# A second pair of token groups by block products one chunk earlier, and a last output tile in halves

## The chip, the cores and the metric

The kernel runs on one core of a Trainium2 chip. The metric is the device time of one launch in microseconds (us). Shorter is better. The engines are called PE (TensorE), DVE (VectorE), ACT (ScalarE), POOL (GpSimd) and SP (SyncE, which here only issues transfers).

## The reference

Attention under a block mask, then two feed-forward stages in float32. The change touches the last one alone:

```python
def _moe2_ref(x, g_ln, w_ch1, w_ch2):          # x: 4 x 576 x 512, w_ch1: 512 x 2048, w_ch2: 2048 x 512
    mu = np.mean(x, axis=-1, keepdims=True)
    var = np.mean((x - mu) ** 2, axis=-1, keepdims=True)
    xn = (x - mu) / np.sqrt(var + 1e-06) * g_ln
    ch = np.maximum(xn @ w_ch1, 0.0) @ w_ch2
    return (x + ch).astype(np.float32)
```

## The kernel before

A float32 matrix product is made as three passes over float32r operands: each operand is split into a high part and a low part (rounded value and remainder), and high x high, low x high and high x low are added up in PSUM.

**The last stage** has 2304 tokens in five groups: four of 512 tokens and one, Z, of 256. The hidden width of 2048 is cut into eight chunks `c` of 256 columns. For each chunk and group, `em_c1` makes the first product (weights `w_ch1`, 24 matmuls of the group's width), ACT takes the relu and DVE the remainder, and `em_c2` makes the second product, one output tile of 128 tokens at a time: six matmuls of 512 columns into a PSUM bank `po` (there are three), which DVE adds to the tile `acc` in SBUF (line 896). In the last chunk each `acc` tile is stored right behind that addition.

**Seven products.** Two groups of 512 tokens form a pair: P is groups 0 and 3, Q is groups 2 and 1. The first product of a pair and a chunk can be seen as a 2x2 block matrix times a 2x2 block matrix. `em_c1s` does it with seven block products of six matmuls (42) in place of eight (48), with sums of the inputs (`SF`, four tiles s0 to s3, each with high and low parts and two halves k) and sums of the weight blocks (`TF`, tiles ta and tb, high part 0 and low part 1). It goes through two plain products, s0 with weight sums, s3 with a plain weight block, s1 with weight sums, then the output tiles of the group before, s2 with weight sums, two output tiles, and a plain input block with weight sums. Its results are put together by three ACT copies and four DVE additions.

**The sums of the inputs** don't depend on the chunk. POOL makes them (`sum_forms`: f1, f2, f3, f4 for s0, s1, s2, s3; 5, 4, 5 and 4 operations for one half k). SBUF holds one pair's `SF` at a time; the other's are kept in DRAM (`s_scr`). Those of P are made in chunks 0 and 1. P goes by seven products from chunk 2 on, Q from chunk 5 on, and in chunks 2 to 4 Q goes plainly by `em_c1`. In these three chunks `sums_for` (line 1320) makes Q's sums a part at a time: when P's seven products are through, the buffer of `TF` is given to POOL as scratch, POOL writes its sums over a part of P's in `SF`, stores them to `s_scr`, loads P's part back, and only then the buffer can take the weight sums of the next chunk. From chunk 5 on `em_c1s` reloads the other pair's `SF` behind each product (`reload`, 1 MB each); chunk 6 has its own second buffer for the weight sums (`TF[6]`, tb).

**What sets the order.** The order is written out by hand; each engine takes its instructions as they stand. Loading and splitting a chunk's weights is cut into steps (`chunk_jobs`, a list of turns). `tick` takes one turn at fixed places among the matmuls. A chunk with one pair by seven products has 17 ticks, one with two has 16. In the list, `forms` makes the four weight sums, `t_high` (ACT) their high part and `t_low` (DVE) the low part; `high` and `low` are the same for a weight piece. Four empty turns stand ahead of the list where the chunk at hand is 2, 3 or 4.

Of the kernel before, what the change touches and what calls it, by code (L numbers as in the profile page):

```python
# [7 lines left out]
F32 = mybir.dt.float32  # L8
# [4 lines left out]
ALU = mybir.AluOpType  # L13
# [10 lines left out]
NC2 = DFF2 // CF  # L24
# [8 lines left out]
def attention_moe_kernel(ctx, tc, raw_d, dup_d, raw0_d, dup0_d, v_d, v0_d, msk_d, mz_d, vec_d, eye_d, wk_d, wv_d, wr_d, wc1_d, wc2_d, out_d):  # L33
    nc = tc.nc
# [327 lines left out]
    def mm(out, lhsT, rhs, start, stop=True, **kw):  # L362
        nc.tensor.matmul(out=out, lhsT=lhsT, rhs=rhs, start=start, stop=stop, **kw)  # L363
# [275 lines left out]
    W = [None, None]  # L639
    TF, XN, SF = {}, {}, []  # L640

    def chunk_jobs(c):
        L, kept = [], []
        for k in (0, 2):
            w = wc1_d[128 * k:128 * k + 256, CF * c:CF * c + CF].rearrange("(a p) n -> p a n", a=2)
            L.append(load_split(w, lambda i, k=k: W[c % 2][0][i][:, k:k + 2], kept))
        for k in range(2):
            r0 = CF * c + 128 * k
            L.append(piece(wc2_d[r0:r0 + 128], lambda i: W[c % 2][1][i], k))
        if c == 0:  # L650
            return L
        z = []

        def forms():
            (b11, b12), (b21, b22) = [[st["a2"].rearrange("p (a n) -> p a n", a=2)[:, :, o:o + 128] for o in (0, 128)] for st in kept]
            raw = stg2.tile([128, 4096], I8, name="raw8")
            z.append(raw.bitcast(F32).rearrange("p (i a n) -> p i a n", i=4, a=2))
            z1, z2, z3, z4 = [z[0][:, i] for i in range(4)]
            for out, in0, in1 in ((z1, b12, b11), (z3, b22, b12), (z2, b22, z1), (z4, b21, z2)):
                tt(out=out, in0=in0, in1=in1, op=ALU.subtract)  # L660

        load, above, below, expo, bits, high, low = [list(x) for x in zip(*[(l, a1, a2, x, b, h, w) for l, (a1, a2), (x, b), h, w in L])]
        low = [lambda f=f: f(nc.vector) for f in low]
        if c == 1:
            return [
                [load[0], load[1]],
                [above[0], below[0]],
                [expo[0], bits[0]],
                [high[0], above[1], below[1], load[2]],
                [expo[1], bits[1]],  # L670
                [high[1], above[2], below[2], low[0], load[3]],
                [expo[2], bits[2]],
                [low[1], high[2], above[3], below[3]],
                [expo[3], bits[3]],
                [low[2], high[3]],
                [low[3]],
            ]
        t_high, t_low = lambda: act(TF[c][0], z[0]), lambda: sub(nc.vector, TF[c][1], z[0], TF[c][0])
        return [
            [load[0], load[1]],  # L680
            [above[0], below[0]],
            [expo[0], bits[0]],
            [high[0], above[1], below[1], load[2]],
            [expo[1], bits[1]],
            [high[1], above[2], below[2], low[0], load[3]],
            [expo[2], bits[2]],
            [forms, above[3], below[3], high[2]],
            [expo[3], bits[3], t_high],
            [low[1], low[2]],
            [high[3], t_low],  # L690
            [low[3]],
        ]

    def chunk_tiles(p):
        return [p.tile([128, 4, CF], F32R, name=f"c1{i}") for i in range(2)], [p.tile([128, 2, DM], F32R, name=f"c2{i}") for i in range(2)]
# [112 lines left out]
    def dma_sums(pr, out, ii, k=slice(0, 2)):  # L808
        for i in ii:
            m, s = s_scr[PAIRS.index(pr), i][:, :, k], SF[i][:, :, k].bitcast(F32)  # L810
            nc.gpsimd.dma_start(out=m if out else s, in_=s if out else m)
# [69 lines left out]
        split(w, 0, b)  # L881
        em_c2(c, g0, (2, 3))

    def em_c2(c, G, ts):
        t0, n = groups[G]
        h1 = T["h1", c, G]
        w2 = W[c % 2][1]
        for t in ts:
            if t >= n // 128:
                continue  # L890
            i = t0 // 128 + t
            p = po.tile([128, 512], F32, name="po")
            for x, (hi_, wi) in enumerate(((0, 0), (0, 1), (1, 0))):
                for m in range(2):
                    mm(p, h1[hi_][:, m, 128 * t:128 * t + 128], w2[wi][:, m], m == 0 and x == 0, m == 1 and x == 2)
            tt(out=acc[i], in0=p, in1=acc[i], op=ALU.add)  # L896
            if c == NC2 - 1:
                nc.sync.dma_start(out=out_d[128 * i:128 * i + 128], in_=acc[i])

# [11 lines left out]
    with tc.manual_schedule():  # L913
# [376 lines left out]
        def open_sums(pr):  # L1290
            T["et"] = ExitStack()
            return sum_forms(pr, opened(T["et"], "tz", 4, side=R))
# [20 lines left out]
        def forms_for(*cc):  # L1313
            T["et"].close()
            T["ef"] = ExitStack() if len(cc) == 1 else es_f
            ta = tf_tiles(opened(T["ef"], "ft", side=R), "ta")
            for c in cc:
                TF[c] = ta

        def sums_for(c):  # L1320
            del TF[c]
            T["ef"].close()
            f1, f2, f3, f4, _ = open_sums(Q)
            if c == 2:
                for k in (0, 1):
                    f3(k)
            else:
                for f in (f1, f2, f4):
                    f(c - 3)
            ii, k = ((2,), slice(0, 2)) if c == 2 else ((0, 1, 3), c - 3)  # L1330
            for pr, out in ((Q, True), (P, False)):
                dma_sums(pr, out, ii, k)
            forms_for(*((c + 1,) if c < 4 else (5, 7)))

        def tick():
            if turns:
# [13 lines left out]

        for c in range(1, NC2):
            if c + 1 < NC2:
                more = chunk_jobs(c + 1)
                if c == 1:
                    turns[0:0] = turns1
                    turns += [[] for _ in range(15 - len(turns))]
                    for x, t in enumerate(more):
                        turns[3 + x] = turns[3 + x] + t
                else:
                    turns += [[] for _ in range(4 * (c < 5))] + more  # L1360
            if c == 1:
                for G in (P[1], P[0], Z, *Q):
                    todo = group(c, G, todo)
                continue
            one, two = (Q, P) if c == 6 else (P, Q)
            em_c1s(c, one, two if c > 4 else None, [lambda ts=ts, x=todo: em_c2(*x, ts) for ts in ((0, 1), (2, 3))], tick)
            if c < 5:
                sums_for(c)
            tick()
            todo = group(c, Z, (c, one[1]))  # L1370
            if c < 5:
                for G in Q:
                    todo = group(c, G, todo)
            else:
                em_c1s(c, two, None, [lambda: em_c2(c, Z, (0, 1))], tick)
                todo = c, two[1]
                tick()
            if c == 4:
                del XN[g3, 0], T["o1"]
                es_o.close()  # L1380
                TF[6] = tf_tiles(opened(es_f, "fb"), "tb")
        em_c2(*todo, range(4))


# [64 lines left out]
```

## Time and profile before

| | us |
|---|---|
| median of three runs | 830.64 (829.98 to 833.07) |
| the profiled execution, its own time | 830.76 |
| its span | 828.9 |
| PE busy in it | 799.6 |
| DVE, ACT, POOL busy | 560.7, 413.9, 333.5 |
| chunks 2 to 7 of the last stage | from about 532 to the end |

The share of busy time is an average over stages. In the last stage PE takes a matmul of 512 columns every 0.23 us almost without a gap, so this stage is read by where PE stands at a time and by what must have arrived by then.

### The profile page before, as it was taken

The page shows a single profiled execution, that of the slowest core. Times are in us where ns is not written, and L with a number is a line of the kernel's source. Part 1 is how long each engine was busy: PE and PEld are TensorE (multiplying, and loading weights), DVE is VectorE, ACT ScalarE, POOL GpSimd, SP SyncE. Part 2 cuts the span into 40 slices and gives each one's busy share as a digit, 9 for nine tenths or more (in the row PEclk, how much of TensorE's full clock was granted, in tenths as well). Part 3 has the DMA queues.
Part 4 walks back from the last instruction along what each step waited for, and adds up shares of the span by engine and source line. Part 5 has one row for each costly group of instructions (what it writes and reads, how often), then busy time and mean ns, then how long its engine had stood idle before and what let it go on. Part 6 is the DMA issues. An engine that isn't in the chain of part 4 may idle for free.

```text
span 828.9 us, 10597 instructions
## 1 busy us (share of the span) xinstructions
PE 799.6 (96%) x3774; PEld 662.9 (80%) x3774; DVE 560.7 (68%) x1014; ACT 413.9 (50%) x706; POOL 333.5 (40%) x294
## 2 busy tenths in 40 slices
PE   4999899899999999999999999999999999999998
PEld 3766766678898998998988887888888888878886
DVE  6898799886788324144386669768576667758545
ACT  6887688878786533535544423233241335243211
POOL 5796789857574011011021669442080730010100
PEclk9999999999999999999999999999999999999999
DMA  8998788721351110012434111604034166160433
GB/s 221 321 338 235 223 253 256 232 94 77 126 211 45 52 64 29 10 39 77 153 110 157 51 52 52 253 26 173 6 113 141 51 207 249 52 239 16 152 153 127
DMA packets 47636, 112.60 MB, mean 136 GB/s; under 512 B 5408, under 2 KB 19872, under 8 KB 45280
## 3 DMA queue, kind: packets, MB, share of 16 engines
q1 hardware_dynamic: 37792, 64.40, 24.2%
q0 software_dynamic: 9360, 45.17, 16.1%
q10 hardware_dynamic: 432, 2.36, 0.7%
q8 instruction: 30, 0.49, 0.2%
q14 instruction: 22, 0.18, 0.1%
HBM read 91.62 MB, written 20.30 MB: 135 GB/s over the span
## 4 chain that ended last, share of the span: by engine, by line
PE 79%; DVE 12%; ACT 5%; issue 2%; DMA 1%; POOL 0%; ACTq 0%; DVEq 0%
PE s L363 23%; PE ph L363 22%; PE po L363 21%; PE p L363 12%; DVE part L418 4%; ACT r L41 2%; ACT e L41 1%; DVE QK L451 1%; DVE a L135 1%; PE ph L714 1%; DMA V<-in_v_dram 1%; DVE acc L896 1%; DVE m L449 1%; DMA raw<-in_raw_dram 1%; ACT h L41 1%
## 5 line engine op out<-in xcount | busy, mean ns | idle before, releaser
L363 PE MATMUL po<-c,h 128*128 128x512 f32 x864 | 207.9, 393 | 1.4 <-DVE acc L896 0.8
L363 PEld LDWEIGHTS po<-c,h 128*128 128x128 f32 x864 | 161.0, 188 | 39.3 <-DVE acc L896 5.0
L363 PE MATMUL ph<-x,c 128*128 128x512 f32 (+1 forms) x552 | 116.6, 353 | 0.0
L896 DVE TENSOR_TENSOR acc<-po,acc 128x512 f32<-128x512 f32 x144 | 94.6, 684 | 23.3 <-PE po L363 22.5
L363 PEld LDWEIGHTS ph<-x,c 128*128 128x128 f32 x552 | 91.4, 188 | 15.3
L363 PE MATMUL p<-e,V 128*128 128x512 f32 (+1 forms) x310 | 91.1, 441 | 0.0
L363 PE MATMUL p<-wv,k 128*128 128x512 f32 x360 | 82.9, 390 | 0.0
L363 PEld LDWEIGHTS p<-e,V 128*128 128x128 f32 x310 | 55.3, 192 | 31.8 <-issue 26.9
L363 PEld LDWEIGHTS p<-wv,k 128*128 128x128 f32 x360 | 67.4, 188 | 13.8
L41 ACT ACTIVATE h<-ph 128x512 fp32r<-128x512 f32 (+1 forms) x53 | 28.3, 534 | 89.1 <-PE ph L363 89.1
L44 DVE TENSOR_TENSOR k<-a,k 128x768 fp32r<-128x768 f32 x24 | 23.0, 958 | 72.2 <-ACT a L41 72.2
L418 DVE TRANSPOSE_TENSOR_REDUCE part<-s 128x14 f32<-128x448 f32 (+4 forms) x160 | 65.1, 467 | 2.7 <-PE s L363 1.8
L41 ACT ACTIVATE a<-raw,ce 128x512 f32<-128x512 int8 (+1 forms) x76 | 54.7, 753 | 17.5 <-DVE a L135 10.9
L41 ACT ACTIVATE u<-ph 128x512 f32<-128x512 f32 x27 | 16.1, 598 | 87.5 <-PE ph L363 86.2
L41 ACT ACTIVATE e<-s 128x1536 f32<-128x1536 f32 (+1 forms) x34 | 48.4, 1424 | 15.3 <-PE s L363 10.1
L363 PE MATMUL s<-y,wk 128*128 128x384 f32 x288 | 51.4, 338 | 0.0
L363 PE MATMUL s<-x,wk 128*128 128x384 f32 x288 | 51.2, 338 | 0.0
L363 PEld LDWEIGHTS s<-y,wk 128*128 128x128 f32 x288 | 50.7, 188 | 0.5 <-DVE r L629 0.3
L363 PEld LDWEIGHTS s<-x,wk 128*128 128x128 f32 x288 | 50.8, 188 | 0.2
L814 POOL DMA_DIRECT2D s<-s_scr x12 | 6.4, 535 | 107.9 <-PE ph L363 107.9
L41 ACT ACTIVATE a<-s 128x768 f32<-128x768 f32 x24 | 19.5, 813 | 58.6 <-PE s L363 58.6
L44 POOL TENSOR_TENSOR kq<-raw,kq 64x512 fp32r<-64x512 f32 x31 | 40.1, 1293 | 21.3 <-DMA kq<-in_dup_dram 15.8
(177 smaller groups left out, 1388.9 us busy)
## 6 DMA issues: line engine op xcount, KB each, us to landing
kq<-in_dup_dram POOLq DMA_DIRECT2D x15, 1088.0 KB, 6.9
s<-s_scr POOLq DMA_DIRECT2D x13, 1024.0 KB, 7.4
raw<-in_raw_dram SPq DMA_DIRECT2D x32, 288.0 KB, 5.7
raw<-in_w_ch_dram SPq DMA_DIRECT2D x16, 511.6 KB, 3.6
raw<-in_w_ch_dram SPq DMA_DIRECT2D x32, 255.6 KB, 3.6
V<-in_v_dram SPq DMA_DIRECT2D x16, 320.0 KB, 5.6
s_scr<-s POOLq DMA_DIRECT2D x5, 1024.0 KB, 6.3
x_scr<-r SPq DMA_DIRECT2D x18, 256.0 KB, 2.0
```

The lines of the kernel that those rows point to most:

```text
L41: nc.scalar.activation(out=out, in_=in_, func=func, **kw)
L44: eng.tensor_tensor(out=out, in0=in0, in1=in1.bitcast(F32), op=ALU.subtract)
L135: stt(out=st["a2"].bitcast(I32), in0=w3, scalar=5, in1=st["a1"].bitcast(I32), op0=ALU.logical_shift_right, op1=ALU.bitwise_or)
L363: nc.tensor.matmul(out=out, lhsT=lhsT, rhs=rhs, start=start, stop=stop, **kw)
L418: red(out=pt[0:kp, b0:b0 + w // 32, j], in_=v3(s[0:kp, o:o + w]), axis=AX.X, op=ALU.max, apply_transpose=True)
L449: lambda: red(out=m, in_=r4[0:32, :, 0:ng], axis=AX.X, op=ALU.max),
L451: lambda x=x: tt(out=v3(dst)[:, x:x + 16], in0=m[:, x:x + 16].unsqueeze(2).to_broadcast([32, 16, 32]), in1=s[64:96, 512:544].unsqueeze(1). ...
L714: nc.tensor.transpose(out=pt[kk][:, 128 * x:128 * x + 128], in_=z[:, 128 * kk:128 * kk + 128], identity=eye)
L814: nc.gpsimd.dma_start(out=SF[i].bitcast(F32), in_=s_scr[PAIRS.index(pr), i])
L896: tt(out=acc[i], in0=p, in1=acc[i], op=ALU.add)
```

## The change

Chunk 4 does both pairs by seven products, as chunks 5 to 7 did before. So Q's sums have to be done in chunks 2 and 3: `sums_for` makes all four sums of one half k in each of them, in the order s0, s1, s3, s2, and stores each as it is done; P's part of each is loaded back one step later. The weight sums of chunks 3 and 4 (`late`) are split at the end of the list, in turns 12 and 13, since POOL holds their buffer longer. The second buffer tb now serves chunks 5 and 7, and the pair that comes first is Q in chunks 5 and 7. In the last chunk the last output tile is made, added and stored in two halves of 256 columns.

```diff
@@ chunk_jobs(c, late=False)
-            [expo[3], bits[3], t_high],
+            [expo[3], bits[3]] + [t_high] * (not late),
             [low[1], low[2]],
-            [high[3], t_low],
-            [low[3]],
-        ]
+            [high[3]] + [t_low] * (not late),
+            [low[3]] + [t_high] * late,
+        ] + [[t_low]] * late
@@ em_c2(c, G, ts, halves=())
+            cols = (slice(0, 256), slice(256, 512)) if t in halves else (slice(0, 512),)
+            for y in cols:
+                p = po.tile([128, 512], F32, name="po")[:, y]
...
+                tt(out=acc[i][:, y], in0=p, in1=acc[i][:, y], op=ALU.add)
+                if c == NC2 - 1:
+                    nc.sync.dma_start(out=out_d[128 * i:128 * i + 128, y], in_=acc[i][:, y])
@@ sums_for(c)
-            if c == 2:
-                for k in (0, 1):
-                    f3(k)
-            else:
-                for f in (f1, f2, f4):
-                    f(c - 3)
-            ii, k = ((2,), slice(0, 2)) if c == 2 else ((0, 1, 3), c - 3)
-            for pr, out in ((Q, True), (P, False)):
-                dma_sums(pr, out, ii, k)
-            forms_for(*((c + 1,) if c < 4 else (5, 7)))
+            for i, f, back in ((0, f1, ()), (1, f2, (0,)), (3, f4, (1,)), (2, f3, (3, 2))):
+                f(c - 2)
+                dma_sums(Q, True, (i,), c - 2)
+                dma_sums(P, False, back, c - 2)
+            forms_for(*((3,) if c == 2 else (4, 6)))
@@ the loop over chunks
-                more = chunk_jobs(c + 1)
+                more = chunk_jobs(c + 1, c in (2, 3))
...
-                    turns += [[] for _ in range(4 * (c < 5))] + more
+                    turns += [[] for _ in range(4 * (c < 4))] + more
...
-            one, two = (Q, P) if c == 6 else (P, Q)
-            em_c1s(c, one, two if c > 4 else None, ...
-            if c < 5:
+            one, two = (Q, P) if c in (5, 7) else (P, Q)
+            em_c1s(c, one, two if c > 3 else None, ...
+            if c < 4:
                 sums_for(c)
...
-            if c == 4:
+            if c == 3:
...
-                TF[6] = tf_tiles(opened(es_f, "fb"), "tb")
-        em_c2(*todo, range(4))
+                TF[5] = TF[7] = tf_tiles(opened(es_f, "fb"), "tb")
+        em_c2(*todo, range(4), (3,))
```

On PE, in chunk 4, where Q's first group begins (x_3733 and x_3734 are its high and low inputs, c_3726 and c_3727 the chunk's weights), before:

```order
L363 MATMUL ph<-x_3733,c_3726 128x512 x4
L363 MATMUL ph<-x_3733,c_3727 128x512 x4
L363 MATMUL ph<-x_3734,c_3726 128x512 x4
L363 MATMUL ph<-x_3733,c_3726 128x512 x4
L363 MATMUL ph<-x_3733,c_3727 128x512 x4
L363 MATMUL ph<-x_3734,c_3726 128x512 x4
```

and with the change (s_3908 is s0, s_3732 is s3, ta_5376 and ta_5377 the weight sums):

```order
L363 MATMUL ph<-x_3733,c_3726 128x512 x2
L363 MATMUL ph<-x_3733,c_3727 128x512 x2
L363 MATMUL ph<-x_3734,c_3726 128x512 x2
L363 MATMUL ph<-x_3733,c_3726 128x512 x2
L363 MATMUL ph<-x_3733,c_3727 128x512 x2
L363 MATMUL ph<-x_3734,c_3726 128x512 x2
L363 MATMUL ph<-s_3908,ta_5376 128x512 x2
L363 MATMUL ph<-s_3908,ta_5377 128x512 x2
L363 MATMUL ph<-s_3908,ta_5376 128x512 x2
L363 MATMUL ph<-s_3732,c_3726 128x512 x2
L363 MATMUL ph<-s_3732,c_3727 128x512 x2
L363 MATMUL ph<-s_3732,c_3726 128x512 x2
```

The plain products of whole groups have become block products, which read s0 and s3 of Q and the weight sums of chunk 4.

On POOL, at the end of its work in chunk 3 (t are scratch tiles; a row with s on the left of s_scr's arrow is a store, the other way round a load), before:

```order
L44 TENSOR_TENSOR s3_3732<-t_5336,s3_3732 128x512
L811 DMA s_scr_78<-s0_3908 256x1x512
L811 DMA s_scr_78<-s1_3909 256x1x512
L811 DMA s_scr_78<-s3_3732 256x1x512
L811 DMA s0_3908<-s_scr_78 128x2x512
L811 DMA s1_3909<-s_scr_78 128x2x512
L811 DMA s3_3732<-s_scr_78 128x2x512
```

and with the change:

```order
L44 TENSOR_TENSOR s3_3732<-t_5355,s3_3732 128x512
L811 DMA s_scr_78<-s3_3732 256x1x512
L811 DMA s1_3909<-s_scr_78 128x2x512
L765 TENSOR_TENSOR t_5363<-x201_3734,o1_3917 128x512
L765 TENSOR_TENSOR t_5362<-x200_3733,o1_3917 128x512
L765 TENSOR_TENSOR t_5362<-t_5362,t_5363 128x512
L777 TENSOR_SCALAR s2_3910<-t_5362 128x512
L44 TENSOR_TENSOR s2_3910<-t_5362,s2_3910 128x512
L811 DMA s_scr_78<-s2_3910 256x1x512
L811 DMA s3_3732<-s_scr_78 128x2x512
L811 DMA s2_3910<-s_scr_78 128x2x512
```

The sum s2 now stands between the store of s3 and the load that brings P's s3 back, and the three loads no longer stand together.

On ACT, at the end of chunk 3 (raw_5470 and raw_5495 hold the weight sums, c_3728 is a weight piece of chunk 4), before:

```order
L41 ACTIVATE c_3728<-a_5431 128x512
L41 ACTIVATE ta_5351<-raw_5470 128x1024
L41 ACTIVATE h_5499<-ph 128x512 x2
L41 ACTIVATE c_3728<-a_5477 128x512
L41 ACTIVATE u<-ph 128x512
```

and with the change:

```order
L41 ACTIVATE c_3728<-a_5456 128x512
L41 ACTIVATE h_5523<-ph 128x512 x2
L41 ACTIVATE c_3728<-a_5502 128x512
L41 ACTIVATE ta_5376<-raw_5495 128x1024
L41 ACTIVATE u<-ph 128x512
```

The high part of the weight sums has moved behind the last weight split, to the place in front of the next chunk's first copy `u`.

## Rows read from the trace of the kernel before

**Rows 1.** The page's head: span, and PE's busy time, share and instructions.

```profile
span 828.9 us, 10597 instructions
PE 799.6 (96%) x3774; PEld 662.9 (80%) x3774; DVE 560.7 (68%) x1014; ACT 413.9 (50%) x706; POOL 333.5 (40%) x294
```

**Rows 2.** Waits of PE's weight loads, 520 to 829 us: total, times, longest.

```profile
PEld po L363 <- DVE acc L896: 3.7, 8, 0.5
```

**Rows 3.** Timeline of PE, chunks 4 and 5: start, us, line, operation, out<-in, count.

```profile
629.00 2.92 PE L363 MATMUL ph<-x,c 128*128 128x512 f32 x12
631.76 1.54 PE L363 MATMUL ph<-s,ta 128*128 128x512 f32 x6
633.13 1.52 PE L363 MATMUL ph<-s,c 128*128 128x512 f32 x6
...
658.33 5.62 PE L363 MATMUL ph<-x,c 128*128 128x512 f32 x24
...
677.47 2.91 PE L363 MATMUL ph<-x,c 128*128 128x512 f32 x12
...
706.92 2.93 PE L363 MATMUL ph<-x,c 128*128 128x512 f32 x12
...
724.90 2.92 PE L363 MATMUL ph<-x,c 128*128 128x512 f32 x12
```

**Rows 4.** Instructions by form, 520 to 829 us: busy us, mean ns | idle before.

```profile
L363 PE MATMUL ph<-x,c 128*128 128x256 f32 x144 | 18.0, 281 | 0.0
...
L741 DVE SCALAR_TENSOR_TENSOR h<-ph,h 128x256 fp32r<-128x256 f32 x12 | 4.9, 418 | 2.3 <-ACT h L41 2.1
```

**Rows 5.** Timeline of POOL, chunk 2 (550) and chunk 3 (598 on).

```profile
550.48 2.58 POOL L765 TENSOR_TENSOR t<-x,o 128x512 f32<-128x512 f32 x2 [23.78 <-PE ph L363]
...
557.12 2.58 POOL L765 TENSOR_TENSOR t<-x,o 128x512 f32<-128x512 f32 x2
...
598.95 2.58 POOL L765 TENSOR_TENSOR t<-o,x 128x512 f32<-128x512 f32 x2 [29.13 <-PE ph L363]
...
605.60 2.67 POOL L765 TENSOR_TENSOR t<-t,x 128x512 f32<-128x512 f32 x2
...
610.95 1.84 POOL L765 TENSOR_TENSOR t<-x,t 128x512 f32<-128x512 f32 x1
...
616.87 2.14 POOL L811 DMA_DIRECT2D s_scr<-s  x3
```

**Rows 6.** The same view in chunk 1, P's second half of sums.

```profile
505.39 3.49 POOL L765 TENSOR_TENSOR t<-s,x 128x512 f32<-128x512 f32 x2
...
512.96 3.29 POOL L765 TENSOR_TENSOR t<-t,x 128x512 f32<-128x512 f32 x2
```

**Rows 7.** Transfers of the whole span: count, KB each, median us from issue to landing.

```profile
raw<-in_w_ch_dram SPq DMA_DIRECT2D x32, 255.6 KB, 3.6
...
s<-s_scr POOLq DMA_DIRECT2D x6, 512.0 KB, 7.9
...
n_scr<-RT SPq DMA_DIRECT2D x7, 16.0 KB, 1.7
```

**Rows 8.** The same view, 549 to 580 us alone.

```profile
s<-s_scr POOLq DMA_DIRECT2D x1, 1024.0 KB, 5.2
```

**Rows 9.** The transfers of `s_scr`, 598 to 632 us; the least is the first store's.

```profile
DMA to landing us min/median/max: 3.2/6.4/9.0
```

**Rows 10.** Timeline of ACT at the start of chunk 4; idle before it in brackets.

```profile
630.58 0.60 ACT L41 ACTIVATE u<-ph 128x512 f32<-128x512 f32 x1 [5.75 <-PE ph L363]
```

**Rows 11.** Timeline of DVE at the start of chunk 4.

```profile
629.20 0.69 DVE L896 TENSOR_TENSOR acc<-po,acc 128x512 f32<-128x512 f32 x1 [0.64 <-PE po L363]
632.03 0.69 DVE L852 TENSOR_TENSOR u<-ph,u 128x512 f32<-128x512 f32 x1 [2.14 <-PE ph L363]
```

**Rows 12.** Timeline of DVE at the end of the kernel.

```profile
825.08 0.69 DVE L896 TENSOR_TENSOR acc<-po,acc 128x512 f32<-128x512 f32 x1 [0.67 <-PE po L363]
```

**Rows 13.** Instructions on the tile `acc`, 800 to 829 us: its stores.

```profile
DMA to landing us min/median/max: 2.0/2.0/4.0
```

More of the change, by code (lines that the diff above doesn't have):

```diff
@@ L640, in attention_moe_kernel, with chunk_jobs @@
     TF, XN, SF = {}, {}, []
-    def chunk_jobs(c):
+    def chunk_jobs(c, late=False):
         L, kept = [], []
@@ L882, in em_c1s, with em_c2 @@
         em_c2(c, g0, (2, 3))
-    def em_c2(c, G, ts):
+    def em_c2(c, G, ts, halves=()):
         t0, n = groups[G]
@@ L891, in em_c2 @@
             i = t0 // 128 + t
[L892 to L898, printed above, removed]
+            cols = (slice(0, 256), slice(256, 512)) if t in halves else (slice(0, 512),)
+            for y in cols:
+                p = po.tile([128, 512], F32, name="po")[:, y]
+                for x, (hi_, wi) in enumerate(((0, 0), (0, 1), (1, 0))):
+                    for m in range(2):
+                        mm(p, h1[hi_][:, m, 128 * t:128 * t + 128], w2[wi][:, m, y], m == 0 and x == 0, m == 1 and x == 2)
+                tt(out=acc[i][:, y], in0=p, in1=acc[i][:, y], op=ALU.add)
+                if c == NC2 - 1:
+                    nc.sync.dma_start(out=out_d[128 * i:128 * i + 128, y], in_=acc[i][:, y])
     PIECES = [
@@ L1364, in attention_moe_kernel @@
                 continue
-            one, two = (Q, P) if c == 6 else (P, Q)
-            em_c1s(c, one, two if c > 4 else None, [lambda ts=ts, x=todo: em_c2(*x, ts) for ts in ((0, 1), (2, 3))], tick)
-            if c < 5:
+            one, two = (Q, P) if c in (5, 7) else (P, Q)
+            em_c1s(c, one, two if c > 3 else None, [lambda ts=ts, x=todo: em_c2(*x, ts) for ts in ((0, 1), (2, 3))], tick)
+            if c < 4:
                 sums_for(c)
@@ L1370, in attention_moe_kernel @@
             todo = group(c, Z, (c, one[1]))
-            if c < 5:
+            if c < 4:
                 for G in Q:
```

## The prediction

> **What bounds the kernel now.** The page comes first: TensorE (PE) is busy 799.6 of 828.9 us [rows 1]. The waits view of the last stage comes next, for the engine's weight loads, where its stalls show: 3.7 us in eight pieces, none over 0.5 us, all for VectorE freeing an output bank [rows 2]. So in this stage the time is the number of matmuls times their pace, and any other engine matters only where it makes PE wait. The PE timeline then gives the pace [rows 3]. Chunk 4 runs from 629.00 to 677.47, 48.47 us; chunk 5, which already does both pairs by seven products, from 677.47 to 724.90, 47.43 us. The reader should note in it where a chunk first reads a sum or a weight sum: 631.76 (first sums times weight sums) and 633.13 (fourth sums, called s3, times a plain weight block). These two times are the deadlines of everything that the change puts at the end of the chunk in front. Last I read the GpSimd (POOL) timeline of chunks 2 and 3 and the landing times of the transfers, since the change loads that engine and its queue.
>
> **Part 1: pair Q in chunk 4 by seven products.** The plain pair takes 48 matmuls, the seven products 42. Before, from 658.33 to 677.47 (the Q part of chunk 4) there are 84 matmuls with the output tiles between them, 19.14 us, 0.228 us each; the same part of chunk 5, from 706.92 to 724.90, has 78 in 17.98 us, 0.2305 each [rows 3]. That is 1.16 us less by this stretch and 1.04 us less by whole chunks, against 6 x 0.228 = 1.37 us if every matmul kept the plain pace; the rest goes to the slightly slower pace of the form. I take 1.04, since chunk 4 will be in the order that chunk 5 has now, with everything that the form adds: three ScalarE copies, four VectorE additions and four reloads of 1 MB on POOL's queue. All of that is thus paid for in the 47.43 us. Chunks 5 to 7 keep their counts; only which pair comes first is swapped, which I cost at nothing. The weight sums of chunks 5 and 7 now go to the second buffer, also nothing.
>
> **Part 2: sums by halves in chunks 2 and 3.** This is where it can be lost. Before, POOL makes 10 operations in chunk 2, 13 in chunk 3 and 13 in chunk 4; now 18 in chunk 2, 18 in chunk 3 and none in chunk 4. It can start only when PE has read the last weight sum, because the scratch tiles lie in that buffer: 598.95 in chunk 3. The four sums take, from the starts of neighbouring rows, 6.65 (605.60 less 598.95), 5.35, 5.92 and, for the one of chunk 2, 6.64 us [rows 5]: 24.6 us. In between stand five DMA issues of about 0.7 us (the three in a row at 616.87 take 2.14 [rows 5]), 3.6 us. So the last sum is done at 598.95 + 24.6 + 3.6 = 627.1, ten us later than the 616.87 of before. Then come the store of that sum (to 627.8), the reload of s3 (issued 627.8) and the reload of s2, which waits for the store in front of it.
>
> Who waits for that? First, the high half of the next weight sums on ScalarE needs the third operation of the last sum, about 624.4. The change puts it behind the last weight split, where ScalarE now idles 5.75 us before its next work at 630.58 [rows 10]. One operation of about 1 us fits there and nothing behind it is late. Second, the low half on VectorE now stands behind the last output addition, 629.20 + 0.69, and so ends about 631.1 (its 1.2 us estimated as twice a 128x512 operation). Behind it VectorE has nothing until 632.03 [rows 11]; PE wants it two matmuls after 631.76, at 632.2. Free, with 1.1 us to spare. Third, the staging buffer that the low half reads is freed some 5 us later, and the next load of weights on SP's queue with it: issued 631.1, median 3.6 us [rows 7], so there by 635. Chunk 4 reads it after 54 matmuls, 629.0 + 54 x 0.228 = 641.3. Free. Fourth, and closest, s3: its reload of 512 KB is issued at 627.8 and PE wants it at 633.13, so 5.3 us are left. No row shows such a load alone. The nearest rows are the 1 MB load with nothing beside it, 5.2 us [rows 8], which is the same kind at twice the size; below, the fastest 512 KB store, 3.2 us [rows 9]; above, the 512 KB loads as they are now, three in a batch with weights beside them, median 7.9 us [rows 7]. Now it has one store in front of it and, until the low half of the weight sums is done, no weights beside it. I take 4.2, between 3.2 and 5.2: there at 632.0, 1.1 us early. So 0 for each of the two boundaries (chunk 2 to 3 and 3 to 4), with 2.6 us each at 7.9. A gain is excluded, since PE has no wait there today. The reload of s2 is issued about 631, and its product stands behind 30 + 24 matmuls, 12 us into the chunk: at 7.9 us it is still in time.
>
> The DMA page of the Trainium skill ("DMA: Bandwidth & Descriptors", section "Anatomy of one DMA") gives about 2.0 us plus the bytes at 436 GB/s for a transfer that GpSimd issues: an estimate of 3.2 us here. The store's 3.2 us agrees with it, the loads' 7.9 us do not. By that rule s3 is there at 631.0 and the slow rival below would be gone; I keep the rival for the row's sake.
>
> **Part 3: the last output tile in halves.** It replaces 6 matmuls of 512 columns by 12 of 256. Those of 256 columns take 18.0 / 144 = 0.125 us each [rows 4], so 1.50 against 1.37 us; if they kept the plain pace, half of 0.228, nothing: I take +0.07. The last addition (825.08, 0.69 us [rows 12]) becomes one of 128x256, nearest row 0.418 [rows 4]: -0.27. The last store of 256 KB lands after 2.0 us [rows 13], one of 16 KB after 1.7 [rows 7]: 0 to -0.3 for 128 KB, I take -0.1. The first half's addition and store lie beside the second half's matmuls. Sum -0.30, from -0.57 to -0.14.
>
> **The sum.** -1.04 + 0 - 0.30 = -1.34 us. The profiled execution took 830.76 us (span 828.9 and 1.86 around it), so 829.42; the median of the runs shown is 830.64, 0.12 lower: 829.3 us.
>
> **Rivals.** (a) POOL's sums take longer because they now lie beside more VectorE work. For it: the same first sum took 7.57 us in the crowded stretch of chunk 1 (505.39 to 512.96 [rows 6]) against 6.65. Nearly 0.9 more for one sum, half of that for each of the others: some 2 us in all. Then s3 arrives at 634.0, PE waits 0.9 us at each boundary, +1.8: 831.1 us. Against it: by 617 most of a chunk's VectorE work is done. The page "SBUF — State Buffer" of the Trainium skill (section "SBUF: two separate sides") states that a VectorE operation with two SBUF inputs and a GpSimd operation that reads SBUF take the shared port pair by an exclusive lock, the other blocking for the whole instruction. The longer sum agrees with that; by the rule this rival is likelier the more VectorE work lies after 617. (b) The slow one: the reload of s3 takes what reloads take now, 7.9 us, so 635.7 and a wait of 2.6 us at two boundaries, +5.2, which eats the gain: 834.5 us; with (a) on top 4.6 each, 838.5. The place is the product of PE's 633.13 row, in chunk 4 and in chunk 3; it begins to cost from 5.3 us on and turns the change slower than before from 6.0. For it: the 7.9 row. Against it: the batch, which is now broken up. (c) The change doesn't do what it says: six matmuls go, but the second pair's chain of additions holds PE up by as much; then only the halves remain, 830.3. Against it: chunks 5 to 7 don't show this.
>
> **How the numbers follow.** Forecast 0.62, (a) 0.20, (b) 0.12, (c) 0.06. The range goes from the forecast with all bounds at their best (1.37 and 0.57 off, 828.7, and half a us of scatter, as the three runs show) to past (a), 828.2 to 832.4 us; (b) is left out. About 0.5% (4.2 us) is what a measurement of this kernel can tell from no change. No bound of the sum gives that much, so faster 0.03; slower is most of (b), 0.11; within 0.86.
>
> **What would show it.** Right: chunk 4 at about 47.4 us, chunks 2 and 3 unchanged (within 0.3), POOL done with its sums about 10 us later in chunk 3, and the last addition 0.4 us long. Wrong at part 2: a PE gap at the s3 product in chunk 3 or 4, released by a DMA, or in front of the first weight-sum product, released by VectorE. Wrong at part 1: a second pair in chunk 4 that takes longer than 18 us.

## The result, and the profile after

The changed kernel is slower: median 836.09 us (833.81 to 837.87, nine runs) against 830.66 us for the kernel before (829.98 to 836.37, nine runs). The ratio is 1.0056, 95% interval 1.0042 to 1.0071, so 3.5 to 5.9 us more. 829.3 us had been forecast and 828.2 to 832.4 as the range.

The page of the changed kernel shows as much work on PE as [rows 1] in a longer span:

```profile
span 835.8 us, 10624 instructions
PE 798.8 (96%) x3774; PEld 661.6 (79%) x3774; DVE 577.3 (69%) x1019; ACT 416.2 (50%) x709; POOL 337.4 (40%) x300
```

DVE is busy 16.6 us longer with five instructions more. The waits from 520 us to the end are the answer to [rows 2]; PE itself, which did not wait at all there before, now has a row, and the longest wait of its weight loads has grown from 0.5 to 2.9 us:

```profile
PE po L363 <- DVE acc L898: 4.7, 2, 2.4
PEld po L363 <- DVE acc L898: 9.6, 11, 2.9
```

The timeline of PE, as in [rows 3], places the two waits. Each stands in front of the last output tile of a chunk, 2 and 3, and the next row is the start of the chunk behind it; the last row is the start of chunk 5:

```profile
584.95 1.66 PE L363 MATMUL po<-c,h 128*128 128x512 f32 x6 [2.44 <-DVE acc L898]
586.45 2.91 PE L363 MATMUL ph<-x,c 128*128 128x512 f32 x12
...
636.14 1.66 PE L363 MATMUL po<-c,h 128*128 128x512 f32 x6 [2.27 <-DVE acc L898]
637.64 2.90 PE L363 MATMUL ph<-x,c 128*128 128x512 f32 x12
...
684.94 2.91 PE L363 MATMUL ph<-x,c 128*128 128x512 f32 x12
```

With chunk 2 starting at 535.26, chunks 2, 3 and 4 take 51.19, 51.19 and 47.30 us (48.48, 48.58 and 48.47 before): two chunks lose 2.7 and 2.6 us, one gains 1.17. From the start of chunk 2 to the end of the span it is 300.5 us against 296.96, 3.6 us more. Below, this stretch is called **the stage** and read beside the ratio, since the time ahead of chunk 2, where the order of PE's work was not changed, scatters: four executions without the change's sums start chunk 2 between 530.65 and 532.67 us.

Now the timeline of DVE in chunk 2, first three rows of the kernel before, at the same work:

```profile
570.84 0.68 DVE L131 TENSOR_TENSOR a<-a,a 128x512 int32<-128x512 f32 x1
571.55 0.69 DVE L135 SCALAR_TENSOR_TENSOR a<-raw,a 128x512 int32<-128x512 int32 x1
...
573.64 1.28 DVE L44 TENSOR_TENSOR c<-a,c 128x512 fp32r<-128x512 f32 x2
```

and the changed kernel:

```profile
575.30 1.28 DVE L898 TENSOR_TENSOR acc<-po,acc 128x512 f32<-128x512 f32 x2
576.50 2.61 DVE L131 TENSOR_TENSOR a<-a,a 128x512 int32<-128x512 f32 x1
579.15 1.67 DVE L135 SCALAR_TENSOR_TENSOR a<-raw,a 128x512 int32<-128x512 int32 x1
580.74 0.68 DVE L741 SCALAR_TENSOR_TENSOR h<-ph,h 128x512 fp32r<-128x512 f32 x1
581.34 2.36 DVE L44 TENSOR_TENSOR c<-a,c 128x512 fp32r<-128x512 f32 x2
583.62 0.68 DVE L741 SCALAR_TENSOR_TENSOR h<-ph,h 128x512 fp32r<-128x512 f32 x1
584.22 1.27 DVE L898 TENSOR_TENSOR acc<-po,acc 128x512 f32<-128x512 f32 x2
```

and POOL in the same microseconds, on the last of its four sums:

```profile
575.98 2.58 POOL L765 TENSOR_TENSOR t<-x,o 128x512 f32<-128x512 f32 x2
578.64 1.63 POOL L765 TENSOR_TENSOR t<-t 128x512 f32<-128x512 f32 x1
580.37 0.93 POOL L777 TENSOR_SCALAR s<-t 128x512 fp32r<-128x512 f32 x1
581.38 1.77 POOL L44 TENSOR_TENSOR s<-t,s 128x512 fp32r<-128x512 f32 x1
583.45 0.71 POOL L811 DMA_DIRECT2D s_scr<-s  x1 [0.30 <-POOL s L44]
584.08 0.73 POOL L811 DMA_DIRECT2D s<-s_scr  x1
...
586.92 0.73 POOL L811 DMA_DIRECT2D s<-s_scr  x1 [2.11 <-DMA s_scr<-s]
```

Two kinds of DVE rows are to be told apart. L898 and L741 read one operand from PSUM and keep their 0.68 us. L131, L135 and L44 split the next chunk's weights, read both operands from SBUF, and are long (2.61, 1.67 and 2.36 us for 0.68, 0.69 and 1.28). Each of them ends 0.55 us after a POOL operation (579.11 after 578.56, 580.82 after 580.27, 583.70 after 583.15), so it seems to run when POOL lets go. The output additions are queued behind them, and PE has only three banks `po`.

The last output tile did become halves, as the DVE timeline at the end shows (it answers to [rows 12]):

```profile
830.89 1.14 DVE L898 TENSOR_TENSOR acc<-po,acc 128x512 f32<-128x512 f32 x2 [0.67 <-PE po L363]
832.32 0.42 DVE L898 TENSOR_TENSOR acc<-po,acc 128x256 f32<-128x256 f32 x1 [0.29 <-PE po L363]
```

### The profile page after: what moved, and what is told of

It is laid out like the page before. It is cut to its first block, busy times and chain, and to the rows that moved or that the text cites. A ratio compares the mean times of both kernels' runs of the same rounds, so it can differ in the third digit from the quotient of the medians.

```text
span 835.8 us, 10624 instructions
## 1 busy us (share of the span) xinstructions
PE 798.8 (96%) x3774; PEld 661.6 (79%) x3774; DVE 577.3 (69%) x1019; ACT 416.2 (50%) x709; POOL 337.4 (40%) x300
## 3 DMA queue, kind: packets, MB, share of 16 engines
q10 hardware_dynamic: 432, 2.36, 0.7%
## 4 chain that ended last, share of the span: by engine, by line
PE 63%; DVE 19%; ACT 9%; issue 4%; DMA 3%; POOL 2%; ACTq 0%; SPq 0%; DVEq 0%; POOLq 0%
PE ph L363 20%; PE po L363 19%; PE s L363 11%; PE p L363 11%; DVE part L418 3%; DVE a L135 3%; DVE mix L553 2%; ACT r L41 2%; DMA raw<-in_raw_dram 2%; ACT e L41 1%; DVE a L131 1%; ACT p L41 1%; DMA raw<-in_w_r_dram 1%; DVE acc L898 1%; ACT a L41 1%
## 5 line engine op out<-in xcount | busy, mean ns | idle before, releaser
L363 PE MATMUL po<-c,h 128*128 128x512 f32 (+1 forms) x870 | 208.6, 391 | 6.2 <-DVE acc L898 5.6
L363 PE MATMUL ph<-x,c 128*128 128x512 f32 (+1 forms) x528 | 110.2, 352 | 0.0
L898 DVE TENSOR_TENSOR acc<-po,acc 128x512 f32<-128x512 f32 (+1 forms) x145 | 94.5, 680 | 19.2 <-PE po L363 17.7
L363 PEld LDWEIGHTS ph<-x,c 128*128 128x128 f32 x528 | 86.9, 188 | 14.4
L44 DVE TENSOR_TENSOR k<-a,k 128x768 fp32r<-128x768 f32 x24 | 23.0, 958 | 72.7 <-ACT a L41 72.7
L814 POOL DMA_DIRECT2D s<-s_scr x16 | 8.5, 534 | 147.2 <-PE ph L363 147.2
L41 ACT ACTIVATE h<-ph 128x512 fp32r<-128x512 f32 (+1 forms) x50 | 26.4, 528 | 78.9 <-PE ph L363 78.9
L41 ACT ACTIVATE u<-ph 128x512 f32<-128x512 f32 x30 | 17.9, 597 | 86.7 <-PE ph L363 81.4
L135 DVE SCALAR_TENSOR_TENSOR a<-raw,a 128x512 int32<-128x512 int32 x47 | 50.6, 1076 | 2.1
L44 POOL TENSOR_TENSOR kq<-raw,kq 64x512 fp32r<-64x512 f32 x31 | 40.1, 1293 | 23.0 <-DMA kq<-in_dup_dram 11.3
```

Of the source, the lines that this page charges most:

```text
L41: nc.scalar.activation(out=out, in_=in_, func=func, **kw)
L44: eng.tensor_tensor(out=out, in0=in0, in1=in1.bitcast(F32), op=ALU.subtract)
L135: stt(out=st["a2"].bitcast(I32), in0=w3, scalar=5, in1=st["a1"].bitcast(I32), op0=ALU.logical_shift_right, op1=ALU.bitwise_or)
L814: nc.gpsimd.dma_start(out=SF[i].bitcast(F32), in_=s_scr[PAIRS.index(pr), i])
L898: tt(out=acc[i][:, y], in0=p, in1=acc[i][:, y], op=ALU.add)
```

## The experiments

Four theories stood to be told apart. **L**: DVE's operations with two SBUF inputs wait for POOL's operations that read, and so the output additions come late. **W**: the loss comes from where the change puts the split of the weight sums (`late`, turns 12 and 13). **R**: the reload of s3 is late as well, hidden behind the bank wait, or is the cause itself. **S**: the microseconds ahead of chunk 2 are scatter and not the program. Each run is compared with runs of the kernel before on the same chip.

**The kernel before, once more** (no edit).

> The kernel before, unchanged, to see how much the part ahead of chunk 2 scatters. In the profile of before the first matmul of chunk 2 starts at 531.94 us, in that of the change at 535.26, though nothing ahead of it was changed. Theory S (scatter of the attention stage): ratio 1.000 within 0.002, and chunk 2 starts anywhere from 531 to 536. Theory P (the changed program itself makes the early part longer): chunk 2 starts at 532 within 0.5. Chunks 2 and 3 take 48.5 us each, chunk 4 48.5.

Measured: ratio 1.0012 (0.9994 to 1.0030), stage 297.05 us (296.96 in the first profile), chunk 2 from 530.65 instead of 531.94. The stage repeats within 0.1 us; the time ahead of it moves by 1.3 us from one execution of a kernel to the next. So some of the 3.3 us between 531.94 and 535.26 is scatter; whether all is, as theory S has it, this run does not show.

**The tail alone**: the kernel before with the last tile in halves (the diff of `em_c2` and its last call).

> The kernel before with the last output tile in halves and nothing else. By the sum of the prediction -0.14 to -0.57 us, ratio 0.9993 to 0.9998: the last addition 0.42 us, its store landing 1.7 to 2.0 us after its issue. A loss would show as a last tile that takes over 1.8 us on TensorE.

Measured: ratio 1.0005 (0.9989 to 1.0021), too coarse for it; the stage takes 296.37 us, 0.6 to 0.7 less. The last addition takes 0.42 us and the span ends 2.75 us behind it, 3.13 before.

**The late weight split alone**: the kernel before with `chunk_jobs(c + 1, c in (2, 3))`.

> The kernel before with the split of the weight sums of chunks 3 and 4 moved to the end of their lists (turns 12 and 13), the sums of the inputs as before. Theory L (VectorE falls behind because its operations with two SBUF inputs wait for GpSimd's operations, which now last 10 us longer into the chunk): no loss, chunks 2 and 3 at 48.5 us within 0.3, ratio 1.000. Theory W (the new place of the split holds VectorE or ScalarE up and through them TensorE): chunks 2 and 3 at 50 to 51 us, ratio 1.003 to 1.006.

Measured: ratio 1.0001 (0.9989 to 1.0014), stage 296.93 us. Theory W is out for the late split by itself; the last version below keeps that split and loses nothing by it.

**Without the sum s2**: the changed kernel, with 13 of POOL's 18 operations in chunks 2 and 3.

```diff
-                f(c - 2)
+                if i != 2:
+                    f(c - 2)
```

> The change without the operations of the last sum (s2) of pair Q on GpSimd in chunks 2 and 3; its store and the reloads stay, and Q's products use what lies in s2, so the output is not the reference's. GpSimd is through some 8 us earlier. Theory L: VectorE's splits after that run at their old durations (0.7 us where the change has 1.7 to 2.6), the two TensorE waits of 2.3 to 2.4 us for a freed output bank are gone or under 0.5 us, chunks 2 and 3 at 48.5 to 49, chunk 4 at 47.3, ratio 0.997 to 1.000. Theory W: the two waits stay, ratio 1.004 to 1.006.

Measured: ratio 0.9984 (0.9969 to 0.9999), stage 295.05 us, chunks 48.49, 48.61 and 47.33. The bank waits are gone, and L131 and L135 behind POOL's last operation (it ends at 572.2) are back at 0.68 and 0.69 us. The loss thus hangs on the fourth sum, but this run takes away three things at once: reading, POOL's time, and the lateness of the reload.

**The changed kernel, once more** (no edit).

> The change itself once more, beside the others of this call, to see what of its loss lies ahead of chunk 2 and what behind. Theory L and theory W alike: from the first matmul of chunk 2 to the end of the span about 300.5 us against 297.0 for the kernel before (two waits of 2.3 to 2.4 us again), while the first matmul of chunk 2 starts anywhere between 530 and 536 us. If the early part were longer because of the change, it would start at 535 again.

Measured: ratio 1.0055 (1.0038 to 1.0072), stage 300.5 us, bank waits of 2.39 and 2.26 us. The loss repeats.

**s2 without reading**: the five operations of s2 become 14 memsets, which write SBUF tiles and read none (P's sum s2 stays as it was).

```diff
-            both(block(g0, 0, k), block(g1, 0, k), ALU.subtract)
-            split(2, k, st.pop("z"))
+            if pr == PAIRS[0]:
+                both(block(g0, 0, k), block(g1, 0, k), ALU.subtract)
+                split(2, k, st.pop("z"))
+                return
+            for x in range(6):
+                z = pool.tile([128, 512], F32, name="t")
+                g.memset(z, 0.0)
+                g.memset(z, 1.0)
+            for x in (0, 1):
+                g.memset(SF[2][:, x, k].bitcast(F32), 0.0)
```

> The change with the five GpSimd operations of the last sum (s2) of pair Q in chunks 2 and 3 replaced by fourteen that only write a constant into scratch tiles and into s2 (so the output is not the reference's), meant to keep GpSimd busy about as long without reading SBUF. Theory L in the form that it is the reading of two operations at once that collides: VectorE's splits in that stretch run at 0.7 us, the TensorE waits for an output bank fall under 0.5 us. Theory L in the wider form that any GpSimd operation holds VectorE up: the waits stay at 2 us or more. Theory R, that behind the bank wait the reload of s3 is late too: once the bank wait is gone, a wait of 0.5 to 1.5 us at the s3 product in chunks 3 and 4, released by a DMA, if GpSimd's last sum ends as late as in the change.

Measured: ratio 1.0053 (1.0030 to 1.0075), and yet the bank waits are gone. First POOL (beginning and end of the memsets, then store and reload), then DVE in chunk 2:

```profile
572.42 0.55 POOL L809 MEMSET t<- 128x512 f32 x1
...
578.75 1.00 POOL L812 MEMSET s<- 128x512 f32 x2
580.04 0.68 POOL L819 DMA_DIRECT2D s_scr<-s  x1 [0.30 <-POOL s L812]
580.64 0.73 POOL L819 DMA_DIRECT2D s<-s_scr  x1
```

```profile
571.77 1.28 DVE L906 TENSOR_TENSOR acc<-po,acc 128x512 f32<-128x512 f32 x2
572.97 0.68 DVE L131 TENSOR_TENSOR a<-a,a 128x512 int32<-128x512 f32 x1
573.68 0.69 DVE L135 SCALAR_TENSOR_TENSOR a<-raw,a 128x512 int32<-128x512 int32 x1
574.29 0.68 DVE L741 SCALAR_TENSOR_TENSOR h<-ph,h 128x512 fp32r<-128x512 f32 x1
574.89 1.28 DVE L44 TENSOR_TENSOR c<-a,c 128x512 fp32r<-128x512 f32 x2
576.10 0.68 DVE L741 SCALAR_TENSOR_TENSOR h<-ph,h 128x512 fp32r<-128x512 f32 x1
576.70 0.68 DVE L906 TENSOR_TENSOR acc<-po,acc 128x512 f32<-128x512 f32 x1
```

POOL is busy until 579.75, with an operation nearly all the time, and DVE's operations beside it have their short times. In both kernels the first of these rows starts 40.0 us into the chunk (571.77 - 531.75 and 575.30 - 535.26); the output addition that follows starts after 44.95 us here and after 48.96 us in the changed kernel. The 4.0 us between are the four longer operations: 2.61 - 0.68, 1.67 - 0.69 and 2.36 - 1.28 make 3.99. PE feels 2.4 of them, the rest was slack. So it is POOL's reading that costs, not its work. A memset is shorter (0.53 us) than an operation of a sum, but a DVE operation that had to wait for even one of them would be longer than 0.68 us, and none is.

In the same run PE waits elsewhere, at the product that reads s3:

```profile
586.72 1.62 PE L363 MATMUL ph<-s,c 128*128 128x512 f32 x6 [2.21 <-DMA s<-s_scr]
...
637.74 1.38 PE L363 MATMUL ph<-s,c 128*128 128x512 f32 x5 [1.96 <-DMA s<-s_scr]
```

Chunk 2 takes 48.48 us, but chunks 3 and 4, which begin with this product, 51.03 and 49.55. Theory R is true behind theory L: once the bank wait is away, the reload is late by about as much, 2.2 and 2.0 us where 0.5 to 1.5 had been expected.

**The weights split four turns earlier**, so that they lie ahead of POOL's last sum.

```diff
-                    turns += [[] for _ in range(4 * (c < 4))] + more
+                    turns += more[:11] + [more[11][:1], [], [], [], more[11][1:], more[12]] if c < 4 else more
```

> The change with the steps that split the next chunk's weights in chunks 2 and 3 four turns earlier (no empty turns ahead of them; only the split of the weight sums stays at the end), so that VectorE has less to do in the last third of the chunk, beside GpSimd's last sum. Theory L: VectorE's operations still stretch beside GpSimd, but not where the output additions are dense; the two TensorE waits fall under 1 us, from chunk 2 to the end 296 to 298 us against 300.5. Theory R: a wait of 0.5 to 1.5 us at the s3 product shows in chunks 3 and 4. Theory W: waits of 2 us or more remain at the end of the chunk.

Measured: a miss. Ratio 1.0081 (1.0056 to 1.0107), stage 303.9 us (296 to 298 expected), chunks 2 and 3 at 53.08 and 52.86 us. The collision went along: POOL has reading operations from 18.5 to 47 us into the chunk, and now other pieces of the split lie beside it. DVE in chunk 3, then PE in chunk 2, whose wait now stands 22 us ahead of the chunk's end, and the row behind that wait:

```profile
611.27 3.49 DVE L660 TENSOR_TENSOR raw<-a,raw 128x256 f32<-128x256 f32 x2
```

```profile
562.34 1.85 PE L363 MATMUL po<-c,h 128*128 128x512 f32 x6 [2.52 <-DVE acc L898]
563.99 7.08 PE L363 MATMUL ph<-x,c 128*128 128x512 f32 x24
```

The bank wait is only a little longer than in the changed kernel, but chunk 2 loses 4.6 us and not 2.7. The second row shows where some 1.5 us more went: 24 such matmuls take 5.62 us elsewhere [rows 3]. From 563.7 to 567.0, behind the 2.5 us in which PE stood still, the granted clock is 0.50, the lower of its two levels (1.2 GHz); in chunk 3 it is 0.50 from 615.4 to 618.1, having fallen within a stop of 2.6 us. Behind the waits of 2.0 to 2.4 us in the changed kernel, in its second run, with memsets and without the load of s3 it stays at 1.00, so it has no part in the loss that is explained here.

**s3 not loaded back** in chunks 2 and 3.

```diff
-                dma_sums(P, False, back, c - 2)
+                dma_sums(P, False, [x for x in back if x != 3], c - 2)
```

> The changed kernel, but P's part of the sum s3 is not loaded back in chunks 2 and 3 (this leaves out a part of the computation; the output is not the reference's). Everything on POOL, VectorE and ScalarE up to the end of the sums stays as in the changed kernel, and the queue behind the last store holds one 512 KB load less. Theory L (VectorE's work with two SBUF inputs waits for POOL's reading sums, the output additions come late): both bank waits in front of the last output tiles of chunks 2 and 3 stay at 2.2 to 2.6 us, chunks 2 and 3 stay at 51.1, the stage from chunk 2 to the end of the span stays at 300.5 us, since the s3 reload is hidden behind the bank wait. Theory R (the reload of s3 is itself the cause of the loss): the stage falls to about 295.5 us, the waits go. Ratio to the kernel before about 1.0055 under L, 0.999 under R.

Measured: ratio 1.0045 (1.0029 to 1.0060), stage 300.44 us, as theory L gave. With one load less the waits are the same:

```profile
583.35 1.65 PE L363 MATMUL po<-c,h 128*128 128x512 f32 x6 [2.44 <-DVE acc L898]
...
634.50 1.68 PE L363 MATMUL po<-c,h 128*128 128x512 f32 x6 [2.26 <-DVE acc L898]
```

So in the changed kernel itself the reload of s3 costs nothing; the bank wait holds PE up until it is there.

**High parts on ACT**: Q's sums are cut into five pieces, and ACT makes the four high parts of each half; POOL keeps 14 operations.

```diff
+        def high(i, k, z):
+            act(SF[i][:, 0, k], z)
+            sub(g, SF[i][:, 1, k], z, SF[i][:, 0, k])
...
@@ sums_for(c)
...
+            first, *rest = open_sums(Q)
+            first(c - 2)
+            for x, f in zip((1, 2, 4, 6), rest):
+                turns[x].insert(0, lambda f=f: f(c - 2))
```

> The changed kernel with the high parts of Q's four sums (one 128x512 rounding copy for each sum and half, four in each of chunks 2 and 3) made by ScalarE instead of POOL, and the sums cut into five pieces that are issued at the place where they began and behind turns 1, 2, 4 and 6 of the list's remaining ticks. POOL is left with 14 operations in place of 18 in each chunk. Theory L with R behind it: POOL is done with reading 24 to 25 us after the chunk's first matmul, as in the run that left one sum out, instead of 29.7; no bank wait over 0.5 us is left, the reload of s3 is issued by 26 us and there in time, chunks 2 and 3 take 48.5 to 48.8 us, chunk 4 keeps 47.3, the stage takes 295.0 us (297.0 in the kernel before), ratio 0.997 to 0.999. If ScalarE's share does not shorten POOL's chain (POOL then waits for ScalarE at each sum), the bank waits stay at 1 to 2 us and the stage at 297 to 299 us.

Measured: ratio 1.0001 (0.9989 to 1.0012), stage 297.2 us, where a failure had been expected to leave it. The bank waits fall to 0.78 and 0.61 us, chunks 2 and 3 to 49.56 and 49.51 (48.5 to 48.8 expected): more than half of the loss is gone. One operation of DVE now takes the worst of it, in chunk 3, and again ends (621.18) 0.55 us after a POOL row, the two `t<-x,o` of 618.05 to 620.63:

```profile
617.70 3.48 DVE L135 SCALAR_TENSOR_TENSOR a<-raw,a 128x512 int32<-128x512 int32 x1
```

**The low parts of s3 and s2 on DVE** too, the last piece one turn earlier; POOL keeps 12 operations.

```diff
-            high(3, k, st["x"])
+            high(3, k, st["x"], nc.vector)
-            high(2, k, st["z"])
+            high(2, k, st["z"], nc.vector)
-            for x, f in zip((1, 2, 4, 6), rest):
+            for x, f in zip((1, 2, 4, 5), rest):
```

> The kernel in which ScalarE makes the high parts (ratio 1.0001), and in chunks 2 and 3 VectorE makes the low parts of the last two sums (s3 and s2) instead of POOL, the last of them one turn earlier. POOL is left with 12 reading operations for each chunk; VectorE has two more with two SBUF inputs, 0.7 us each where POOL is not reading beside them. By theory L what counts is the VectorE work that lies beside POOL's reading in the last third of the chunk: POOL's last reading operation ends about 20 to 21 us after the chunk's first matmul row of POOL work began at 18.5 to 19, that is near 621 in place of 627.8 in chunk 3 of the run before, so L135, L660 and L131 from there on go back to 0.69, 0.41 and 0.68 us. Expected: the bank waits of 0.8 and 0.6 us fall under 0.5, chunks 2 and 3 take 48.5 to 48.8 us (49.5 with ScalarE alone), the stage 295.0 to 295.6 us, ratio 0.997 to 0.999. If the sheer amount of VectorE work counts and not the collision, two more operations make the waits longer: 50 us for each chunk, ratio 1.001 to 1.002.

Measured: ratio 1.0000 (0.9991 to 1.0009), stage 296.4 us (295.0 to 295.6 expected). The bank waits are 0.50 and 0.36 us; chunks 2 and 3 take 49.27 and 49.26 us, better, but not the 48.5 to 48.8 expected. POOL's reading ends at 620.8, as forecast, and from there on L131 and L135 are short (0.68 and 0.69). What was not forecast is that one operation can lose more than before, beside POOL's row of two from 616.52 to 619.10 (it ends at 619.65, again 0.55 later):

```profile
616.01 3.64 DVE L131 TENSOR_TENSOR a<-a,a 128x512 int32<-128x512 f32 x1
```

**The low part of s1 on DVE** as well; POOL keeps 11 operations and makes the last sum ahead of the store of s1.

> As the kernel with two low parts on VectorE, and VectorE makes the low part of s1 too; POOL is left with 11 reading operations for each chunk and makes the last sum ahead of the store of s1. Theory L: POOL's reading ends another 1.8 us earlier, about 619 in chunk 3; VectorE has 0.7 us more work, ahead of 617, where it still idles. Chunks 2 and 3 at 48.5 to 48.7 us, the stage at 295.0, ratio 0.997 to 0.999, equal to the kernel with two within the scatter. If the amount of VectorE work counts: longer waits than with two, ratio 1.002.

Measured: ratio 0.9973 (0.9965 to 0.9982), 828.61 us (12 runs) against 830.96 (23 runs) for the kernel before. This version is faster than the kernel before by 2.2 us (1.5 to 2.9 by the interval), and than the kernel with two low parts on DVE, which it had been expected only to equal. POOL's last operation and first store behind it, then DVE in chunk 3:

```profile
614.46 1.30 POOL L765 TENSOR_TENSOR t<-t 128x512 f32<-128x512 f32 x1
615.69 0.69 POOL L847 DMA_DIRECT2D s_scr<-s  x1
```

```profile
616.23 0.68 DVE L131 TENSOR_TENSOR a<-a,a 128x512 int32<-128x512 f32 x1
616.94 0.69 DVE L135 SCALAR_TENSOR_TENSOR a<-raw,a 128x512 int32<-128x512 int32 x1
...
625.14 1.28 DVE L934 TENSOR_TENSOR acc<-po,acc 128x512 f32<-128x512 f32 x2
```

POOL reads until 615.76, 36.1 us into the chunk, and everything on DVE behind it has its short time, although DVE has six operations more in all. The one row of waits of PE's weight loads is again about that of the kernel before [rows 2], and the chunks are back:

```profile
PEld po L363 <- DVE acc L934: 4.0, 9, 0.5
```

```profile
531.15 2.92 PE L363 MATMUL ph<-x,c 128*128 128x512 f32 x12
...
579.62 2.91 PE L363 MATMUL ph<-x,c 128*128 128x512 f32 x12
...
628.20 2.92 PE L363 MATMUL ph<-x,c 128*128 128x512 f32 x12
...
675.55 2.91 PE L363 MATMUL ph<-x,c 128*128 128x512 f32 x12
```

Chunks 2, 3 and 4 take 48.47, 48.58 and 47.35 us, the stage 294.95. That the sheer amount of DVE's work counts, the other reading of the two runs before, falls with it.

## Why the prediction was wrong

**Part 1 was right.** Chunk 4 became 1.17 us shorter in the changed kernel and 1.12 in the last version; 1.04 had been taken, from [rows 3].

**Part 3 was right in its steps and rather too small.** -0.30 was forecast, -0.57 at best; the tail alone shortened the stage by 0.6 to 0.7. The addition gave the 0.27 of [rows 4] and [rows 12]. What lies behind it (the store and the end) takes 2.74 to 3.10 us in the ten executions with the halves and 3.09 to 3.18 in the three without. It thus gave 0.38 in the run with the tail alone but only 0.07 in the changed kernel; 0.1 had been taken.

**Part 2 is the step that failed.** It took 0 for the two boundaries, with the sentence that a gain was excluded and a loss would come by s3. It is +2.7 and +2.6 us. The waits stand at neither of the two places that it named as signs (the s3 product, the first product with weight sums), but one tile ahead of the boundary, for an output bank. Two things were wrong in it.

First, it asked only who waits for POOL's results. It did not ask whom POOL's work disturbs while it runs. The loss is DVE's: 4.0 us in the last part of a chunk, on operations that have nothing to do with the sums, and through the output additions PE's. Rival (a) had the right two engines with the wrong victim. It took the 0.9 us that one sum of POOL's had lost in [rows 6] as its price, sent it to PE by way of s3, and came to 831.1. The rule was at hand: the prediction cites the exclusive lock of the Trainium skill's page "SBUF — State Buffer", section "SBUF: two separate sides", in which whichever comes second blocks. That can be either engine, and only one was priced. The traces agree with who gets in whose way by the rule: the DVE operations with two SBUF inputs went from 0.68 to as much as 3.64 us beside reading operations of POOL, those with one input in PSUM did not, and memsets that only write left both alone. Who comes first they don't bear out in every case: the operation of 3.64 us has a recorded start 0.5 us ahead of the POOL operations that it outlasted.

The cover was stated and not read, too. "By 617 most of a chunk's VectorE work is done" had no row behind it. In the changed kernel DVE has no idle time that the trace shows between 620.05 and 639.66, and what is queued there are the output additions that PE's banks hang on. DVE's row in the kernel before was looked at behind 629 only [rows 11], where POOL's results were due, and not from 616.87 to 627, where POOL's new work [rows 5] would lie. There the trace of the kernel before shows it busy for 9.90 of the 12.00 us from 617 to 629, more densely than in the stretch in front (9.22 of the 12.60 us from 604.4).

Second, s3. POOL's chain began as forecast (18.5 us into the chunk) and took 29.7 us to the store of the last sum instead of 28.15; its operations are longer beside DVE's too (`t<-t` took 1.29 us in the first sum of chunk 2, 1.63 in the last). The reload landed 5.3 us after its issue in the changed kernel and 5.9 and 6.1 us in the run with memsets; 4.2 had been taken from the nearest rows [rows 8, 9]. (Where a load of this size was issued after the store had landed, in the run without the load of s3, it took 4.1 and 4.3 us; that of s3 is issued 0.6 us behind a store that takes 3.2.) Some 1.5 us from the chain and 1.7 to 1.9 from the reload, less the 1.1 us to spare, make about the 2.2 and 2.0 us that PE is late at this product in the run with memsets. So s3 was late by a part of rival (a), which had given the chain some 2 us, and a part of rival (b), whose reload of 7.9 us did not come; and it came out as no cost, because the bank wait in front covers it. That (b)'s 834.5 us lies near the measured time is luck: its waits at s3 are not those that were measured.

**The sum.** With the stage's own pieces: +2.71 and +2.61 for chunks 2 and 3, -1.17 for chunk 4, -0.17 and +0.09 for chunks 5 and 6, -0.49 for chunk 7 and the end, together +3.58 us. The runs' ratio gives 3.5 to 5.9. What of this lies above 3.6 stays open: nine executions of kernels with the change's sums, in whole or varied, start chunk 2 at 531.15 to 535.26, four without it at 530.65 to 532.67, and that is not enough to tell a small effect ahead of chunk 2 from scatter. With part 2 at the 0 that was forecast the change would have given about 2 us: the last version's stage is 2.0 us shorter than before (-1.12 in chunk 4, -0.79 in chunk 7 and the end, -0.1 for the rest).

## What to carry to other kernels

When work is moved to an engine that "has time", list what the other engines do in the very microseconds in which it will run, and price both directions of a collision, not only the new work's own lateness. On this pair of engines the question for each row is where its operands lie: DVE operations with two SBUF inputs and POOL operations that read SBUF stand in each other's way, while PSUM operands and pure writes do not. And when a wait is found, take away its cause and look for the next one behind it: here a late load that costs about as much was hidden there, and only a version that ended POOL's reading early cured both.

## What the runs showed of the hardware

A DVE operation can lose far more than the one POOL operation it meets: 0.68 us became 3.64 beside two POOL operations of 1.29 us each that follow one another without a gap, and the start that the trace shows for it (616.01) lies ahead of theirs (616.52). Moving two operations from POOL to DVE changed which DVE operation met this, and the gain stayed under what was expected. Fourteen memsets of POOL, 0.5 us each, ran in the same place at no cost to DVE. How the two engines are served in such a meeting, and why the one that began first can be the one that waits, was not tried.

A stop of PE can cost more than the stop itself: at the end of 2.5 and 2.6 us of it in one run the granted clock was 0.50 for about 3 us, at the end of 2.0 to 2.4 us in four others it stayed at 1.00. What tells these cases apart was not tried.
